# Cutting the token dimension of the experts' plain second product unevenly in four groups of one batch

## The chip, the cores and the metric

The kernel runs on one core of one Trainium2 chip. The metric is the device time of one launch in microseconds (us), taken as the median of several runs; lower is better. A run's profile gives a span, from the first instruction to the last, which is a little shorter than the device time.

## The reference, cut to what matters

Three stages follow one another. A memory attention over 4 batches of 576 tokens gives `x` of 2304 tokens by 512 features. A dense layer with a parametrised ReLU follows. The last stage is a mixture of four experts, all of which work on every token:

```python
p = domain_probs / (domain_probs.sum(-1, keepdims=True) + 1e-09)
for e in range(E):                      # E = 4, F = 1024
    h = np.maximum(x @ w1[e], 0.0)
    out += p[:, e:e + 1] * (h @ w2[e])  # h @ w2[e] is the second product
```

The 4 x 1024 hidden features are treated as eight groups of 512 (`NG = 8`), two to an expert. The change concerns `h @ w2[e]` of groups 3, 4, 5 and 6 for batch 1, and nothing else.

## The kernel before, in words

**Layout.** Features lie on the 128 partitions and tokens along the free dimension. A batch has `S = 576` tokens, and `HB = 288` is half of them. Every float32 operand is kept as two parts, a rounded `hi` and the rest `lo`, both of type fp32r, and a product of two operands is made as three matmuls (`PASSES`: hi·hi, hi·lo, lo·hi) which add up in PSUM.

**Order of the work.** The attention and the dense layer follow an order written out by hand (`ORDER`). `run_experts` then goes through 32 units: first batches 0 and 1 in turn for groups 0 to 7, then batches 2 and 3 in turn for groups 0 to 7. The order in which instructions are issued is the order of the Python calls; each engine runs its own in that order. A unit (g, b) computes the first product of its group with a seven-product scheme in two halves (`Up`, `hp` = 0 and 1; products `p1` to `p7`, six matmuls each of 288 columns, 84 in a unit). Between them stand the products of the second matmul for the unit before it: `old.product(n)` and `old.flush(n)`, called through `down`. VectorE builds the blocks of `h` from the products in PSUM (line 840, tiles `v` and `h`), applies the gate (line 884), and ScalarE, GpSimd and VectorE make the `hi` and `lo` parts (tile `g`).

**The plain second product.** Batches 0 and 1 use the class `Down`. Its eight products `n = 0..7` are those of four blocks `d` of 128 output features and two token halves `j`. One product is twelve matmuls into one bank of PSUM (tile `o`, line 914): two `hp`, two halves `i`, three passes. Each of the twelve has another 128 x 128 block of weights, which is loaded into the array by an instruction of its own; the moving operand is the slice `j * HB:(j + 1) * HB` of the 576 tokens of tile `g`. The PSUM pool `ps_h` has two banks, which the products take in turn. `flush(n)` adds the bank to the accumulator in SBUF on VectorE (line 931, tile `acc`), for group 0 by a ScalarE copy (line 929). Of batches 2 and 3 all groups but the last use another scheme (class `Seven`, line 978).

In a unit that hosts `Down`, products 0, 1 and 2 stand in its first half, after `p7`, `p4` and `p3`, and products 3 to 7 in its second half, after `p6`, `p2`, `p7`, `p4` and `p3`. The products of (g, batch 1) are hosted by the unit (g + 1, batch 0). For groups 3 to 6 these are the units that begin at about 592.5, 640.4, 688.1 and 736.2 us.

**Waits that stand around them.** `p4` of a half writes on into the bank that VectorE reads for `v167` (line 871), `p3` into the one that it reads for `c22` (line 874). A product `n + 2` takes the bank of product `n` after its flush.

Of the kernel before, what the change touches and what calls it, by code (L numbers as in the profile page):

```python
# [8 lines left out]
F32 = mybir.dt.float32  # L9
# [7 lines left out]
B, H, S, D, M = 4, 8, 576, 64, 32  # L17
# [4 lines left out]
HB = S // 2  # L22
# [169 lines left out]
def memory_attention_experts(ctx: ExitStack, tc: tile.TileContext, phi, q, kv, w_in, w_out, w1, w2, alpha, dp, out):  # L192
# [16 lines left out]
    ps_h = ctx.enter_context(tc.tile_pool(name="ps_h", bufs=2, space=PSUM))  # L209
# [12 lines left out]
    def unit(name, dt=F32, pool=big):  # L222
        return pool.tile([128, UNIT], dt, tag="big", name=name)
# [398 lines left out]
    xu_t, acc_t, p_t, w1_t, w2_t, g_t = {}, {}, {}, {}, {}, {}  # L622
# [10 lines left out]
    def operand(b, i):  # L633

        n = b % 2 * 7 + i
        if (b // 2, n // 2) not in xu_t:
            xu_t[b // 2, n // 2] = unit(f"x{b}{i}", F32R).rearrange("p (c x k n) -> p c x k n", c=2, x=2, k=2)
        return xu_t[b // 2, n // 2][:, n % 2]
# [155 lines left out]
    class Up:  # L794
# [6 lines left out]
        def product(self, p, a, i, start):  # L801
            w = w1_t[self.g, self.hp].rearrange("p x (c k n) -> p x c k n", c=7, k=2)
            n = 0
            for k in range(2):
                for x, y in PASSES:
                    mm(p, w[:, x, a, k], operand(self.b, i)[:, y, k], start=(start and n == 0), stop=(n == 5), skip_group_check=not start)  # L806
                    n += 1
# [89 lines left out]
    class Down:  # L897


        def __init__(self, g, b):  # L900
            self.g, self.b, self.ps = g, b, {}

        def product(self, n, hps=(0, 1)):
            d, j = divmod(n, 2)
            if 0 in hps:
                self.ps[n] = ps_h.tile([128, 512], F32, tag="h", name=f"o{self.g}{self.b}{n}")[:, 0:HB]
            self.p = self.ps[n]
            m = 6 * hps[0]
            for hp in hps:
                w = w2_t[self.g, hp, d // 2].rearrange("p x (i n) -> p x i n", i=2)  # L910
                for i in (1, 0):
                    for x, y in PASSES:
                        g = g_t[self.g, self.b, hp][:, i, y, j * HB:(j + 1) * HB]
                        mm(self.p, w[:, x, i, d % 2 * 128:(d % 2 + 1) * 128], g, start=(m == 0), stop=(m == 11), skip_group_check=len(hps) == 1)  # L914
                        m += 1

        def flush(self, n):
            d, j = divmod(n, 2)
            g, b = self.g, self.b
            if b > 1:  # L920
                a = acc_t[b][(P2, P3, P4, P5)[d // 2 * 2 + j]][:, d % 2]
                nc.vector.tensor_tensor(out=a, in0=self.p, in1=a, op=ALU.add)
                nc.sync.dma_start(out=out[d * 128:(d + 1) * 128, b * S + j * HB:b * S + (j + 1) * HB], in_=a)
                return
            if n == 0 and g == 0:
                acc_t[b] = unit(f"acc{b}", pool=pools["acc"]).rearrange("p (d n) -> p d n", d=4)
            a = acc_t[b][:, d, j * HB:(j + 1) * HB]
            if g == 0:
                nc.scalar.copy(out=a, in_=self.p)
            else:  # L930
                nc.vector.tensor_tensor(out=a, in0=self.p, in1=a, op=ALU.add)  # L931
            if g < NG - 1:
                return
            if j == 1:
                nc.sync.dma_start(out=out[d * 128:(d + 1) * 128, b * S:(b + 1) * S], in_=acc_t[b][:, d])
# [356 lines left out]
    for kind in ("in", "out"):  # L1292
        for i in range(DFF // 128):
            d = Decode(kind, i)
# [66 lines left out]
```

## Time and profile before

| quantity | value |
|---|---|
| device time, median of 3 runs | 1167.02 us (1165.84 to 1167.2) |
| span of the profiled execution | 1164.3 us |
| TensorE matmul busy | 1142.6 us, 98% of the span |
| VectorE busy | 853.2 us, 73% |
| ScalarE busy | 473.1 us, 41% |
| GpSimd busy | 410.0 us, 35% |
| mean granted clock of TensorE | 0.994 of full |

The profile gives the span of the profiled execution and no device time of its own for it; the median of the runs lies 2.7 us above the span. Engines are named PE (TensorE matmul), PEld (TensorE weight load), DVE (VectorE), ACT (ScalarE), POOL (GpSimd) and SP (SyncE). The duration of one matmul in the profile reaches from its first read to its modelled last write, and matmuls overlap; the pace of a stream is therefore read from the distance of starts.

### The profile page before, as it was taken

The numbers are of one execution on the slowest core, as the hardware profiler recorded it, in microseconds if no ns is written. First come the engines' busy times: TensorE is split into PE (matmuls) and PEld (weight loads), VectorE is DVE, ScalarE is ACT, GpSimd is POOL, SyncE is SP. The second block draws the span as 40 slices with busy tenths as digits, with TensorE's granted clock in tenths as the row PEclk, the third lists the DMA queues.
The fourth block names the chain that finished last, engine by engine and source line by source line (L and its number), as shares of the span: only waits on it lengthen the run. The fifth ranks groups of instructions, "written<-read, shape, count | busy, mean of one in ns | idle before, by whom it ended". The sixth has DMA issues, their size and how long they took to land.

```text
span 1164.3 us, 21801 instructions
## 1 busy us (share of the span) xinstructions
PE 1142.6 (98%) x8628; PEld 1096.0 (94%) x8628; DVE 853.2 (73%) x1573; ACT 473.1 (41%) x1035; POOL 410.0 (35%) x333
## 2 busy tenths in 40 slices
PE   8899999999999989999999999999999999999998
PEld 7578999999999989999999999999999999999998
DVE  6999888885558674767757766678667777777794
ACT  5567756555455534333323333223432222222220
POOL 2333022322010164745646456433333333333320
PEclk9999999999999989999999999999999999999999
DMA  9740221312000262745637455485545556555512
GB/s 375 274 177 20 73 91 55 91 37 82 1 1 1 85 258 104 279 169 212 242 120 296 152 220 227 172 303 197 181 158 189 164 165 185 162 181 182 163 65 72
DMA packets 64214, 180.02 MB, mean 155 GB/s; under 512 B 6640, under 2 KB 23024, under 8 KB 60400
## 3 DMA queue, kind: packets, MB, share of 16 engines
q1 hardware_dynamic: 64112, 178.63, 43.9%
q8 instruction: 68, 1.11, 0.4%
q14 instruction: 34, 0.28, 0.1%
HBM read 114.34 MB, written 64.26 MB: 153 GB/s over the span
## 4 chain that ended last, share of the span: by engine, by line
PE 88%; DVE 7%; DMA 2%; issue 2%; POOL 1%; ACT 1%; SPq 0%; DVEq 0%; ACTq 0%; POOLq 0%
PE o L914 18%; PE y L600 17%; PE c L978 13%; PE uy L806 12%; PE h L562 8%; PE ux L806 8%; PE uw L806 8%; PE pw L523 2%; DMA rawin<-in_w_in 2%; DVE g L232 1%; PE pm L325 0%; POOL g L232 0%; POOL w L232 0%; DVE h L884 0%; DVE g L581 0%
## 5 line engine op out<-in xcount | busy, mean ns | idle before, releaser
L914 PE MATMUL o<-g,w 128*128 128x288 f32 x1536 | 226.0, 296 | 0.7 <-DVE g L232 0.4
L914 PEld LDWEIGHTS o<-g,w 128*128 128x128 f32 x1536 | 211.6, 189 | 1.1 <-DVE g L232 0.6
L600 PE MATMUL y<-g,wout 128*128 128x288 f32 x1440 | 205.5, 297 | 0.0
L600 PEld LDWEIGHTS y<-g,wout 128*128 128x128 f32 x1440 | 194.2, 188 | 10.5 <-issue 7.0
L806 PE MATMUL uy<-x,w 128*128 128x288 f32 x1152 | 186.0, 297 | 3.4 <-DVE v L840 3.4
L806 PEld LDWEIGHTS uy<-x,w 128*128 128x128 f32 x1152 | 163.9, 189 | 6.0 <-DVE v L840 5.9
L978 PE MATMUL c<-gc,w2c 128*128 128x288 f32 x1008 | 156.3, 295 | 0.5 <-ACT acc L991 0.5
L978 PEld LDWEIGHTS c<-gc,w2c 128*128 128x128 f32 x1008 | 141.1, 188 | 1.0 <-ACT acc L991 1.0
L232 POOL TENSOR_TENSOR gc<-h,gc 128x576 fp32r<-128x576 f32 x56 | 83.0, 1490 | 143.0 <-ACT gc L965 99.9
L806 PE MATMUL ux<-x,w 128*128 128x288 f32 x768 | 122.8, 295 | 2.8 <-ACT v L844 2.7
L806 PE MATMUL uw<-x,w 128*128 128x288 f32 x768 | 122.7, 295 | 0.0
L806 PEld LDWEIGHTS ux<-x,w 128*128 128x128 f32 x768 | 108.6, 188 | 3.2 <-ACT v L844 3.2
L965 ACT CAST gc<-h 128x576 fp32r<-128x576 f32 x70 | 47.3, 675 | 152.0 <-DVE h L957 138.6
L562 PE MATMUL h<-a,wp 128*128 128x288 f32 x720 | 108.8, 296 | 0.1
L806 PEld LDWEIGHTS uw<-x,w 128*128 128x128 f32 x768 | 108.8, 188 | 0.0
L232 POOL TENSOR_TENSOR w<-raww,w 128x512 fp32r<-128x512 f32 (+1 forms) x48 | 76.3, 1606 | 86.6 <-ACT w L705 59.8
L562 PEld LDWEIGHTS h<-a,wp 128*128 128x128 f32 x720 | 99.5, 188 | 2.7 <-issue 1.3
L931 DVE TENSOR_TENSOR acc<-o,acc 128x288 f32<-128x288 f32 x112 | 50.8, 454 | 69.2 <-PE o L914 69.2
L581 DVE SCALAR_TENSOR_TENSOR pos<-neg,nal,pos 128x288 f32<-128x288 f32 x120 | 64.8, 544 | 43.0 <-ACT pos L576 42.5
L840 DVE TENSOR_TENSOR v<-uy,v 128x288 f32<-128x288 f32 x128 | 58.1, 454 | 50.7 <-PE uy L806 50.6
L575 ACT ACTIVATE neg<-h 128x288 f32<-128x288 f32 x128 | 53.0, 414 | 83.3 <-PE h L562 78.6
L232 POOL TENSOR_TENSOR g<-pos,g 128x288 fp32r<-128x288 f32 x29 | 24.4, 845 | 173.0 <-ACT g L585 142.8
(163 smaller groups left out, 1670.9 us busy)
## 6 DMA issues: line engine op xcount, KB each, us to landing
kw<-w SPq DMA_DIRECT2D x16, 1792.0 KB, 6.9
raww<-in_w SPq DMA_DIRECT2D x32, 512.0 KB, 3.9
w<-kw SPq DMA_DIRECT2D x32, 512.0 KB, 4.6
kS<-S SPq DMA_DIRECT2D x56, 256.0 KB, 5.0
w2c<-kS SPq DMA_DIRECT2D x28, 512.0 KB, 3.6
kw<-w SPq DMA_DIRECT2D x25, 512.0 KB, 2.7
w<-kw SPq DMA_DIRECT2D x48, 256.0 KB, 3.9
kv<-in_kv SPq DMA_DIRECT2D x8, 1152.0 KB, 12.6
```

Source lines behind the costliest of these rows:

```text
L232: eng.tensor_tensor(out=out, in0=in0, in1=in1.bitcast(F32), op=ALU.subtract)
L523: mm(p[64 * j:64 * j + 64, g * 256:(g + 1) * 256], vt_t[b, g][:, j, :], win_t[c][:, 2 * g + j, e * 256:(e + 1) * 256], start=True, stop=True,)
L562: mm(p, wp_t[b, c, f // 2][:, x, o2 + g * 256:o2 + g * 256 + 128], a_t[b][:, y, g, o:o + HB], start=(n == 0), stop=(n == 5))
L575: nc.scalar.activation(out=neg, in_=p, func=AF.Relu, scale=-1.0)
L581: nc.vector.scalar_tensor_tensor(out=pos, in0=neg, scalar=nal[:, ft:ft + 1], in1=pos, op0=ALU.mult, op1=ALU.add)
L600: mm(First.acc[d], w[:, x, d * 128:(d + 1) * 128], self.gt[:, y, 0:HB], start=(self.start and n == 0), stop=(self.stop and n == 2))
L806: mm(p, w[:, x, a, k], operand(self.b, i)[:, y, k], start=(start and n == 0), stop=(n == 5), skip_group_check=not start)
L840: nc.vector.tensor_tensor(out=out, in0=x, in1=y, op=ALU.add)
L914: mm(self.p, w[:, x, i, d % 2 * 128:(d % 2 + 1) * 128], g, start=(m == 0), stop=(m == 11), skip_group_check=len(hps) == 1)
L931: nc.vector.tensor_tensor(out=a, in0=self.p, in1=a, op=ALU.add)
L965: nc.scalar.copy(out=t[:, 0], in_=self.raw[q])
L978: mm(self.p, w[:, x, i, m * 128:(m + 1) * 128], self.g_t[q][:, y, i], start=(k == 0), stop=(k == 5))
```

## The change

For batch 1 and groups 3 to 6 the two token pieces of every product become unequal: 512 + 64 (group 3), 384 + 192 (group 4), 320 + 256 (group 5) and 448 + 128 (group 6) in place of 288 + 288. The number of products, of matmuls, of weight loads and of flushes stays; so do their order and the tokens covered. Even `n` (`j = 0`) has the wide piece, odd `n` the narrow one.

```diff
+        def tokens(self, j):
+
+            cut = {3: 512, 4: 384, 5: 320, 6: 448}.get(self.g, HB) if self.b == 1 else HB
+            return (cut, S) if j else (0, cut)
+
         def product(self, n, hps=(0, 1)):
             d, j = divmod(n, 2)
+            t0, t1 = self.tokens(j)
             if 0 in hps:
-                self.ps[n] = ps_h.tile([128, 512], F32, tag="h", name=f"o{self.g}{self.b}{n}")[:, 0:HB]
+                self.ps[n] = ps_h.tile([128, 512], F32, tag="h", name=f"o{self.g}{self.b}{n}")[:, 0:t1 - t0]
...
-                        g = g_t[self.g, self.b, hp][:, i, y, j * HB:(j + 1) * HB]
+                        g = g_t[self.g, self.b, hp][:, i, y, t0:t1]
...
-            a = acc_t[b][:, d, j * HB:(j + 1) * HB]
+            a = acc_t[b][:, d, slice(*self.tokens(j))]
```

## Rows read from the trace of the kernel before

**Rows 1.** The page: span, and busy time by engine (share of the span) and instructions
```profile
span 1164.3 us, 21801 instructions
PE 1142.6 (98%) x8628; PEld 1096.0 (94%) x8628; DVE 853.2 (73%) x1573; ACT 473.1 (41%) x1035; POOL 410.0 (35%) x333
```

**Rows 2.** The page: the chain that ended last, share by engine
```profile
PE 88%; DVE 7%; DMA 2%; issue 2%; POOL 1%; ACT 1%; SPq 0%; DVEq 0%; ACTq 0%; POOLq 0%
```

**Rows 3.** The page, costliest groups: busy us, mean ns of one | idle before, releaser
```profile
L914 PE MATMUL o<-g,w 128*128 128x288 f32 x1536 | 226.0, 296 | 0.7 <-DVE g L232 0.4
L931 DVE TENSOR_TENSOR acc<-o,acc 128x288 f32<-128x288 f32 x112 | 50.8, 454 | 69.2 <-PE o L914 69.2
```

**Rows 4.** Windows, the four hosting units: length, busy us (instructions) by engine, granted clock
```profile
core 0: us, PE busy (x) PEld busy (x) DVE busy (x) ACT busy (x) POOL busy (x), PEclk, DMA share, GB/s
592.50:616.40 23.90, 23.90 (x183) 23.90 (x182) 16.01 (x27) 8.06 (x14) 10.86 (x8) 1.00 0.30 102
640.30:664.20 23.90, 23.90 (x183) 23.90 (x182) 15.93 (x27) 8.06 (x14) 10.78 (x8) 1.00 0.25 92
688.00:711.90 23.90, 23.90 (x183) 23.90 (x182) 15.74 (x27) 8.06 (x14) 10.59 (x8) 1.00 0.27 102
735.80:759.70 23.90, 23.90 (x183) 23.90 (x182) 14.93 (x25) 7.86 (x14) 9.78 (x7) 1.00 0.47 170
```

**Rows 5.** Timeline of TensorE matmuls, first hosting unit: start us, length us, instructions
```profile
592.53 0.95 PE L806 MATMUL ux<-x,w 128*128 128x288 f32 x6
...
596.49 1.76 PE L914 MATMUL o<-g,w 128*128 128x288 f32 x12
...
601.26 1.76 PE L914 MATMUL o<-g,w 128*128 128x288 f32 x12
...
610.01 1.74 PE L914 MATMUL o<-g,w 128*128 128x288 f32 x12
611.59 0.96 PE L806 MATMUL uy<-x,w 128*128 128x288 f32 x6
...
616.36 0.95 PE L806 MATMUL ux<-x,w 128*128 128x288 f32 x6
```

**Rows 6.** Timeline of TensorE matmuls after an idle stretch, first plain product
```profile
426.41 3.08 PE L914 MATMUL o<-g,w 128*128 128x288 f32 x12
429.29 1.19 PE L806 MATMUL uy<-x,w 128*128 128x288 f32 x6
```

**Rows 7.** Windows, columns as in rows 4: that product, and its surroundings
```profile
426.40:429.20 2.80, 2.80 (x13) 2.80 (x13) 2.77 (x4) 1.12 (x3) 2.63 (x2) 0.50 0.90 301
...
426.00:450.00 24.00, 24.00 (x170) 24.00 (x170) 13.30 (x19) 9.63 (x21) 15.15 (x13) 0.92 0.73 256
```

**Rows 8.** Groups by form, weight loads of 32, 64 and 128 columns: mean ns
```profile
L914 PEld LDWEIGHTS o<-g,w 128*128 128x128 f32 x1536 | 211.6, 189 | 1.1 <-DVE g L232 0.6 <-ACT acc L929 0.5
...
L523 PEld LDWEIGHTS pw<-win,vt 128*64 128x64 f32 x256 | 15.5, 136 | 10.8 <-issue 5.7 <-DVE pe L362 0.3 <-ACT y L613 0.2
...
L325 PEld LDWEIGHTS pm<-kv,pe 128*32 128x32 f32 x256 | 6.5, 109 | 1.6 <-issue 1.0 <-ACT neg L575 0.5
```

**Rows 9.** Timeline, plain float32 matmuls of 128 columns and their weight loads
```profile
20.32 2.17 PE L246 MATMUL warm<-ident 128*128 128x128 f32 x18
...
20.33 2.09 PEld L246 LDWEIGHTS warm<-ident 128*128 128x128 f32 x18
```

**Rows 10.** Timeline, plain float32 matmuls of 288 columns
```profile
44.77 2.10 PE L597 MATMUL y<-g,wholeout 128*128 128x288 f32 x8
46.71 2.10 PE L559 MATMUL h<-pe,wp 128*128 128x288 f32 x8
```

**Rows 11.** Groups by form, VectorE tensor_tensor of 576 columns
```profile
L664 DVE TENSOR_TENSOR xt<-y 128x576 f32<-128x576 f32 x4 | 3.0, 751 | 0.0
```

**Rows 12.** Timeline of VectorE in the first hosting unit
```profile
598.07 2.03 DVE L232 TENSOR_TENSOR w<-s,w 128x1024 fp32r<-128x1024 f32 x1 [0.36 <-ACT w L705]
600.02 0.45 DVE L931 TENSOR_TENSOR acc<-o,acc 128x288 f32<-128x288 f32 x1
...
610.21 0.46 DVE L840 TENSOR_TENSOR v<-uy,v 128x288 f32<-128x288 f32 x1 [0.33 <-PE uy L806]
```

## The prediction

> **What bounds the kernel now.** I read the page first. TensorE is busy for 1142.6 of 1164.3 us [rows 1], and the chain of work that ended last runs through it for 88% [rows 2]. Those are averages, so the second view was the windows of the four units that host the products to be cut. In each of them TensorE matmuls and weight loads fill all 23.90 us, the granted clock is 1.00 (2.4 GHz), and VectorE, the next engine, is busy for 14.9 to 16.0 us [rows 4]. The reader is to see that nothing waits there: a nanosecond more or less of TensorE work in these units is a nanosecond of the end. The third view was the timeline, for the pace. A unit has 84 matmuls of the first product and 96 of the second, all of 288 columns; the first starts at 592.53, the next unit's first at 616.36 [rows 5]. That is 23.83 us / 180 = 132.4 ns from start to start, though the reported duration of one is 296 ns [rows 3].
>
> **The change, part by part.** Nothing is added or removed: in each of the four groups 96 matmuls stay, 48 of them wide and 48 narrow, with the same 576 columns to a pair. A pair costs 264.8 ns before. So the whole question is the pace as a function of the width.
>
> *The wide piece.* After an idle stretch one product ran at the granted clock 0.50, the 1.2 GHz level [rows 7]: twelve matmuls took 429.29 - 426.41 = 2.88 us, 240 ns each [rows 6], which is 288 columns at one per cycle and nothing more. At 2.4 GHz the columns need 120 ns, so 12.4 of the 132.4 ns are something else. It can be fixed for each matmul, and then the price is N/2.4 + 12.4: 225.7 ns for 512 columns, 199.1 for 448, 172.4 for 384, 145.7 for 320, 119.1 for 256. It can grow with the columns, and then the price is 0.4597 ns a column: 235.4, 205.9, 176.5, 147.1, 117.7. Or it can be that at 288 columns the weight load is already the slower one of the two; then the wide pieces pay only the small excess of the plain float32 rows, where 8 matmuls start over 1.94 us, 242.5 ns each, 2.5 above two turns of 120 [rows 10].
>
> *The narrow piece.* No row shows an fp32r matmul of fewer than 288 columns. What is known is that each needs a new 128 x 128 block of weights. The mean reported load is 109 ns for 32 columns of weights, 136 for 64 and 189 for 128 [rows 8]: (189 - 109)/96 = 0.83 ns a column, so 128 columns stream for about 107 ns and the rest is fixed latency. The nearest row for the pace is the plain float32 stream with only 128 columns to move, 128 weight columns to load, and the clock at 1.00 by then: 18 matmuls in 2.17 us with 0.275 us for the last, 111.5 ns each; the loads, (2.09 - 0.19)/17 = 111.8 ns [rows 9]. So a load can follow a load every 111.7 ns, and I take that as the floor F of a matmul, however narrow. The ends are 107 ns (streaming alone) and 132.4 ns (a narrow matmul no dearer than one of 288). Without a floor, at the fixed price, the narrow pieces would cost 39.1 (64), 65.7 (128) and 92.4 ns (192); these three are raised to F, the 256 of group 5 is not.
>
> *The sum, fixed price and F = 111.7,* 48 pairs to a group:
> group 3: 225.7 + 111.7 - 264.8 = 72.6 ns, 3.48 us;
> group 4: 172.4 + 111.7 - 264.8 = 19.3 ns, 0.93 us;
> group 5: 145.7 + 119.1 - 264.8 = 0;
> group 6: 199.1 + 111.7 - 264.8 = 46.0 ns, 2.21 us;
> together 6.6 us. With the price by the column: 3.95 + 1.12 + 0 + 2.53 = 7.6 us. I take the middle, 7.1 us. The ends: 5.9 us with F = 107 and the fixed price; 10.2 us with F = 132.4 and the fixed price (4.48 + 1.92 + 0.64 + 3.20); the load-bound reading of 288, F = 132.4 and wide pieces at N/2.4 + 2.5, gives 4.00 + 1.44 + 0.16 + 2.73 = 8.3 us, inside them.
>
> The Trainium skill, TensorE: Matmul & The Clock Gate, section LDWEIGHTS, states that a weight load takes its columns divided by 1.2 GHz, which is an estimate of 107 ns for 128 columns; by it alone the sum would be the 5.9 us, and the slope of [rows 8] agrees with it.
>
> *The flushes.* VectorE's add takes 454 ns at 288 columns [rows 3] and a tensor_tensor of 576 takes 751 [rows 11], so 1.03 ns a column and 157 ns fixed: about 685 ns at 512, 223 at 64, together the 908 of before. Its total stays. Where could a longer flush hold a bank? The tightest place is product 0: its flush stood behind a split of 2.03 us, began at 600.02 and ended at 600.47 [rows 12], 0.79 us before product 2 took the bank at 601.26 [rows 5]. In group 3 product 0 ends 1.12 us later and product 2 starts about 0.87 us later (1.12 less the 0.25 that a narrow product 1 saves), while the flush behind the split ends only 0.23 us later: slack 1.4 us. Cost nothing; if that cover were gone, tenths of a microsecond a unit.
>
> *The cover of v167.* In the second half, `p4` at 611.59 [rows 5] needs `v167`, which ended at 610.67 [rows 12]; product 5, narrow now, lies between `p7` and `p4`. Twelve matmuls at F last 1.34 us in place of 1.58, so the slack of 0.92 us falls to 0.68. No new wait. No DMA and no ScalarE work is moved.
>
> **The rivals.**
>
> *No floor: not slower (1167.0).* If loads of weights run far enough ahead, or several are held, the narrow matmul pays only its columns and the 12.4 ns, and each pair costs what it did: 0 us. For it: loads are a separate instruction that overlaps matmuls, and 12.4 ns is all that shows at 288. Against it: weight loads were never closer than 111.7 ns in [rows 9], where something shorter would not have shown, since the matmuls there set nearly the same pace. It decides from F of about 76 ns down: 48 x ((F - 39.1) + (F - 65.7)) ns is then 2.3 us, 0.2% of the time, which is about what a measurement of this kernel can tell from no change. The Trainium skill, same page, section Back-to-back issue gap, gives N/2.4 + 2.5 ns for an isolated matmul and about 25 ns as its least; no pair would change by that rule, and at 288 columns it gives 122.5 ns where the trace has 132.4.
>
> *Faster (1163).* If the 12.4 ns belong to the 288-wide stream and both pieces pay N/2.4 + 2.5, a pair costs 245.0, and 192 pairs save 3.8 us. It needs the absence of a floor as well.
>
> *Narrow fp32r loses its rate (1189).* A plain float32 product needs two matmul instructions, each 242.5 ns at 288 columns [rows 10], 1.68 ns a column together. If an fp32r matmul below some width ran at that price, 192 columns would cost 323 ns and 128 columns 215.6, while 64 (108) stays at F: 3.48 + 11.07 + 0 + 7.19 = 21.7 us. If 256 columns fell under it too, group 5 would add 15.0. For it: no row has a narrow fp32r matmul. Against: nothing in the trace shows fp32r leaving one column per cycle.
>
> *The clock falls (1178 to 1181).* If the grant fell to 1.2 GHz in the narrow products as it did after the idle stretch, each fall costs what 426 to 450 us lost: 170 matmuls in place of 183 or so, 1.7 us [rows 4, 7]. Two to four falls add 3.4 to 6.8. Against: a narrow product lasts 1.34 us and the next work is dense; the trace shows the lower level only after TensorE stood idle.
>
> **How the numbers follow.** The floor between 107 and 132 ns: 0.80, with its own range of 1172.9 to 1177.2, or 1172.2 to 1177.9 with the 0.7 us by which the runs differ. No floor: 0.08. Narrow fp32r at the plain price: 0.07. Clock: 0.03. Faster: 0.02. The forecast is 1167.0 + 7.1 = 1174.1 us; in the profile the span goes from 1164.3 to about 1171.4. The range of 1170.5 to 1179.5 holds the first case, most of the clock case, and floors from about 85 ns; it leaves out some 0.17. Faster by over 0.2%: 0.02; within 0.2%: 0.08; slower: 0.90, from the same cases.
>
> **What would show it.** In the units that host groups 3 to 6, the distance of starts in the products of line 914, by form: some 226 to 235 ns at 512, and the same 107 to 132 ns at 64, 128 and 192, with the loads' distance equal to it. The units should grow by about 3.7, 1.0, 0 and 2.4 us, with TensorE without idle time. Line 931 should have rows near 685 and 223 ns. I am wrong if the narrow starts come at 40 to 90 ns, if 192 columns cost over 300 ns, if the clock falls below 1.00 there, or if TensorE waits for VectorE in these units.

## The result, and the profile after

The changed kernel takes 1172.67 us (median of 3 runs, 1172.14 to 1173.26), 1.0051 of the time before (95% interval 1.0031 to 1.0071). The first medians are 5.65 us apart; five more runs of it, told of below, give 1.0064 (1.0050 to 1.0078), 7.3 us. It is slower by some 7 us, as forecast. The span of the profiled execution went from 1164.3 to 1171.5 us, where 1171.4 had been expected; that this agrees to 0.1 us is partly luck, since the three executions had spans of 1170.4, 1170.9 and 1171.5 us.

The page of the changed kernel, as in [rows 1]: TensorE is busy for 6.2 us more with the same 8628 matmuls.

```profile
span 1171.5 us, 21801 instructions
PE 1148.8 (98%) x8628; PEld 1100.1 (94%) x8628; DVE 851.6 (73%) x1573; ACT 472.9 (40%) x1035; POOL 409.2 (35%) x333
```

Windows of the changed kernel over the hosting units, as in [rows 4], of which the first and the last stand here: TensorE still fills all four, at a granted clock of 1.00. Nothing waits for a longer flush or a shorter cover.

```profile
592.80:620.30 27.50, 27.50 (x182) 25.39 (x180) 15.58 (x27) 8.05 (x14) 11.07 (x8) 1.00 0.27 98
...
740.90:767.10 26.20, 26.20 (x183) 25.44 (x181) 14.39 (x25) 7.85 (x14) 9.75 (x7) 1.00 0.48 177
```

Timeline of TensorE matmuls in the changed kernel: the first matmuls of the hosting units and of the units behind them, and two products of group 3.

```profile
592.80 0.95 PE L806 MATMUL ux<-x,w 128*128 128x288 f32 x6
...
596.77 2.94 PE L920 MATMUL o<-g,w 128*128 128x512 f32 x12
599.55 0.95 PE L806 MATMUL uy<-x,w 128*128 128x288 f32 x6
600.34 1.42 PE L920 MATMUL o<-g,w 128*128 128x64 f32 x12
601.60 1.05 PE L806 MATMUL uw<-x,w 128*128 128x288 f32 x6
602.48 2.94 PE L920 MATMUL o<-g,w 128*128 128x512 f32 x12
...
620.35 1.03 PE L806 MATMUL ux<-x,w 128*128 128x288 f32 x6
...
644.26 0.95 PE L806 MATMUL ux<-x,w 128*128 128x288 f32 x6
...
669.14 0.99 PE L806 MATMUL ux<-x,w 128*128 128x288 f32 x6
...
693.00 0.95 PE L806 MATMUL ux<-x,w 128*128 128x288 f32 x6
...
716.88 0.95 PE L806 MATMUL ux<-x,w 128*128 128x288 f32 x6
...
740.92 0.95 PE L806 MATMUL ux<-x,w 128*128 128x288 f32 x6
...
767.10 1.01 PE L806 MATMUL ux<-x,w 128*128 128x288 f32 x6
```

The same starts in the kernel before, beside the first unit's in [rows 5]; the third hosting unit begins at 688.30 us, not at about 688.1 as said above:

```profile
640.41 0.95 PE L806 MATMUL ux<-x,w 128*128 128x288 f32 x6
...
664.24 0.95 PE L806 MATMUL ux<-x,w 128*128 128x288 f32 x6
...
688.30 0.95 PE L806 MATMUL ux<-x,w 128*128 128x288 f32 x6
...
712.13 0.95 PE L806 MATMUL ux<-x,w 128*128 128x288 f32 x6
...
736.18 0.95 PE L806 MATMUL ux<-x,w 128*128 128x288 f32 x6
...
760.01 0.95 PE L806 MATMUL ux<-x,w 128*128 128x288 f32 x6
```

Each hosting unit took 23.83 us before. Now the one of group 3 (512 + 64) takes 620.35 - 592.80 = 27.55, group 4 (384 + 192) 24.88, group 5 (320 + 256) 23.88, group 6 (448 + 128) 26.18 us: 3.72 + 1.05 + 0.05 + 2.35 = 7.17 us more. The reader is to see two things besides. The wide product of 512 took 599.55 - 596.77 = 2.78 us, 232 ns a matmul. The narrow one took 601.60 - 600.34 = 1.26 us, and the six matmuls behind it 602.48 - 601.60 = 0.88 us in place of 0.79. The trace gives the reason: the first narrow matmul starts at 600.34, the second only 0.03 us later, and from there on they follow every 0.11 us. So the start of a matmul that waits for its weights is reported some 0.08 us before its turn, and the last of the narrow pace falls on the next group. Together 1.35 us, 112 ns a matmul.

And the units between the hosting units got shorter. The first went from 640.41 - 616.36 = 24.05 us to 644.26 - 620.35 = 23.91, the second from 24.06 to 693.00 - 669.14 = 23.86, the third stayed (24.05 and 24.04). Before, the weight loads of each of the three had waited 0.2 us for VectorE (tile `v`, line 840); in the changed kernel one of the three waits is left. From the first start to the last of these rows, the stretch of the four hosting units and the three between, the kernel takes 767.10 - 592.80 = 174.30 us in place of 760.01 - 592.53 = 167.48, so 6.82 us more.

### The profile page after: what moved, and what is told of

Read it like the earlier page. It is cut to its first block, busy times and chain, and to the rows that moved or that the text cites. A ratio compares the mean times of both kernels' runs of the same rounds, so it can differ in the third digit from the quotient of the medians.

```text
span 1171.5 us, 21801 instructions
## 1 busy us (share of the span) xinstructions
PE 1148.8 (98%) x8628; PEld 1100.1 (94%) x8628; DVE 851.6 (73%) x1573; ACT 472.9 (40%) x1035; POOL 409.2 (35%) x333
## 4 chain that ended last, share of the span: by engine, by line
PE 89%; DVE 6%; issue 1%; DMA 1%; POOL 1%; ACT 1%; DVEq 0%; POOLq 0%; ACTq 0%; SPq 0%
PE o L920 18%; PE y L600 17%; PE c L984 13%; PE uy L806 12%; PE h L562 8%; PE uw L806 8%; PE ux L806 8%; PE pw L523 3%; DMA rawout<-in_w_out 1%; PE warm L246 1%; DVE g L232 1%; PE pm L325 1%; POOL g L232 0%; POOL w L232 0%; PE pc L357 0%
## 5 line engine op out<-in xcount | busy, mean ns | idle before, releaser
L920 PE MATMUL o<-g,w 128*128 128x288 f32 (+5 forms) x1536 | 232.7, 300 | 0.7 <-DVE g L232 0.4
L920 PEld LDWEIGHTS o<-g,w 128*128 128x128 f32 x1536 | 215.5, 189 | 3.5 <-DVE g L232 0.6
L937 DVE TENSOR_TENSOR acc<-o,acc 128x288 f32<-128x288 f32 (+4 forms) x112 | 50.9, 454 | 76.1 <-PE o L920 75.9
L844 ACT COPY v<-ux 128x288 f32<-128x288 f32 x64 | 25.6, 400 | 152.1 <-PE ux L806 146.3
```

## The experiments

**The changed kernel again**, five more runs, no edit.

> The changed kernel once more, to narrow its interval. Theory (a matmul costs its columns, but never less than one weight load of about 112 ns): the four hosting units grew by 3.72, 1.05, 0.05 and 2.36 us in its profile and the span by 7.2, so 6.5 to 7.5 us over the kernel before, ratio 1.0056 to 1.0064. If the true gain is nearer the 5.65 us between the medians of the first runs, the ratio is 1.0048.

Measured: 1173.71 us against 1166.42, ratio 1.0064 (1.0050 to 1.0078). That is 7.3 us, inside the interval of the first runs too. The 5.65 us between the first medians (1.0048) lie just below the new interval, which reaches from 5.8 to 9.1 us.

**All four groups 512 + 64.**

```diff
-            cut = {3: 512, 4: 384, 5: 320, 6: 448}.get(self.g, HB) if self.b == 1 else HB
+            cut = {3: 512, 4: 512, 5: 512, 6: 512}.get(self.g, HB) if self.b == 1 else HB
```

> All four groups cut 512+64. Theory (floor of one weight load): each hosting unit grows by the 3.72 us of group 3, together 14.9, less some 0.3 to 0.4 us of waits on VectorE in the units between that go, so about 14.5 us over the kernel before (ratio 1.0124). Rival (the cost comes from the new forms themselves, paid once for each width, or from the clock): not four times group 3, but 4 to 8 us.

Measured: 1180.15 us, ratio 1.0121 (1.0108 to 1.0135), 13.7 us. In its profile each of the four hosting units takes 27.54 us and each unit between 23.92, so that the stretch is 181.92 us, 14.4 more than before: four times group 3 less what the units between give back. It is no cost paid once for a new form.

**All four groups 320 + 256.** The same line with 320 four times.

> All four groups cut 320+256. Theory (floor of 112 ns, 256 columns take 119): nothing, 0 to 0.3 us, ratio 1.0000 to 1.0003. Rival (unequal pieces cost by themselves, through longer flushes or waits for a bank): some tenths of a microsecond in each hosting unit, 1 us or more in all, with TensorE idle before products in the trace.

Measured: 1166.51 us against 1166.42, ratio 1.0000 (0.9991 to 1.0008). Unequal pieces by themselves cost nothing that can be measured, 1 us at most; in the profile the stretch is 167.57 us against 167.48. So the cost lies in pieces narrower than 256.

**Half of the weight columns for the narrow piece.** On top of 512 + 64 in four groups (the line of `mm` is shortened; the run leaves out half of the output features of the narrow pieces):

```diff
+            rows = 64 if t1 - t0 == 64 else 128
...
-                        mm(self.p, w[:, x, i, d % 2 * 128:(d % 2 + 1) * 128], g, ...)
+                        mm(self.p[0:rows], w[:, x, i, d % 2 * 128:d % 2 * 128 + rows], g, ...)
...
+                r = 64 if (g in (3, 4, 5, 6) and b == 1 and j) else 128
-                nc.vector.tensor_tensor(out=a, in0=self.p, in1=a, op=ALU.add)
+                nc.vector.tensor_tensor(out=a[0:r], in0=self.p[0:r], in1=a[0:r], op=ALU.add)
```

> As all four groups cut 512+64, but the matmuls of the 64-token piece take only the first 64 of their 128 weight columns, so 64 of 128 output features of these tokens are left out for groups 3 to 6 of batch 1. Theory (the floor is the loading of the weight columns): the mean reported load is 136 ns for 64 columns and 189 for 128, so the floor falls by about 53 ns to some 58, 48 x 53 ns = 2.6 us less in each group, 4 us over the kernel before in place of 14.5. Rival (a fixed least distance between matmul instructions, whatever they load): still about 14.5 us.

Measured: 1171.80 us, ratio 1.0048 (1.0034 to 1.0061), 5.4 us. The number of matmuls and of columns moved is that of the run with 13.7 us; 61% of the cost went away with half of the weight columns. So the floor is the loading of weights, not a least distance between instructions. Timeline of that kernel, one narrow product and what follows it:

```profile
599.90 0.83 PE L921 MATMUL o<-g,w 128*64 128x64 f32 x12
600.57 1.05 PE L806 MATMUL uw<-x,w 128*128 128x288 f32 x6
```

Twelve starts take 0.67 us where they took 1.26. The next group again takes 0.89 us in place of 0.79 (it ends at 601.46), so a narrow matmul costs 64 ns, where some 58 had been expected; with 232 for the wide one that is 31 ns a pair over the 264.8, or 6.0 us in the four groups before the units between give some back. The 4 us that were expected lie at the edge of the interval.

**Both products of a block back to back, and matmul by matmul in turn.** Again 512 + 64 in four groups. Both products of a feature block are issued at the place of the wide one (a control), or their matmuls alternate (`INTERLEAVED` stands for the choice and is False in the control; `steps(n)` holds the twelve matmuls of product `n`):

```diff
+            if n % 2 == 0:
+                steps = [self.steps(n), self.steps(n + 1)]
+                if INTERLEAVED:
+                    for x, y in zip(*steps):
+                        x()
+                        y()
+                else:
+                    for s in steps:
+                        for x in s:
+                            x()
+            self.p = self.ps[n]
```

> As all four groups cut 512+64, but the two products of a feature block are issued together, the wide one and then the narrow one, at the place of the wide one; the place of the narrow one holds only its flush. A control for the interleaved run. Theory: the same matmuls, so about 14.5 us over the kernel before, perhaps a little more where VectorE waits move.

> The same places, but the two products are issued matmul by matmul in turn, wide, narrow, wide, narrow, with the same block of weights loaded for both. Theory (a block of weights can be loaded only while the one before it is in use, one ahead): the load for the next wide matmul starts when the narrow one starts and lasts longer than it, so each narrow matmul still costs 112 ns and the time is that of the control, about 14.5 us over the kernel before. Rival (loads run ahead and only their mean rate counts): two loads of 112 ns fit under a pair of 232 + 28 ns, the cost goes, and the time is within 1.5 us of the kernel before.

Measured: back to back 1185.79 us, ratio 1.0164 (1.0149 to 1.0179), 19.1 us; in turn 1188.88, ratio 1.0186 (1.0169 to 1.0203), 22.2 us. Both miss the 14.5 us. Taking the matmuls in turn saves nothing, as the theory says, but the places cost more than it said. Timeline of the kernel in turn, one pair of products (24 matmuls) and the two groups around `p7` and `p4`:

```profile
597.46 4.20 PE L937 MATMUL o<-g,w 128*128 128x512 f32 x24
601.50 1.04 PE L806 MATMUL uy<-x,w 128*128 128x288 f32 x6
...
615.22 1.03 PE L806 MATMUL uy<-x,w 128*128 128x288 f32 x6
616.80 1.05 PE L806 MATMUL uy<-x,w 128*128 128x288 f32 x6 [0.55 <-DVE v L840]
```

The same pair in the control:

```profile
596.45 4.21 PE L937 MATMUL o<-g,w 128*128 128x512 f32 x24
600.50 1.04 PE L806 MATMUL uy<-x,w 128*128 128x288 f32 x6
```

A row of this view merges both widths. The twelve pairs took 601.50 - 597.46 = 4.04 us in turn and 600.50 - 596.45 = 4.05 us one product after the other. With the 0.08 us that falls on the next group that is 344 ns a pair, 232 + 112. So a wide matmul of 232 ns ahead of each narrow one does not help, and the rival's 260 ns a pair is refuted. Timeline of the weight loads in turn: the second and the third from the wide matmul at 597.46 us on; the first starts with it.

```profile
597.70 0.19 PEld L937 LDWEIGHTS o<-g,w 128*128 128x128 f32 x1
597.80 0.19 PEld L937 LDWEIGHTS o<-g,w 128*128 128x128 f32 x1
```

While the wide matmul runs one block is loaded, the narrow one's. The load for the next wide matmul starts 0.23 us later, together with the narrow matmul (597.69), and the one after it another 0.11 us later, when that load has come in and the next wide matmul can take its weights (its start is reported 0.08 us early, at 597.72).

What was missed are waits. The waits of TensorE in the kernel in turn, 592 to 790 us (engine, tile, line, waited for: us in total, times, longest):

```profile
PE uy L806 <- DVE v L840: 2.5, 5, 0.6
PE o L937 <- DVE acc L969: 1.8, 4, 0.5
```

With no product between `p7` and `p4`, TensorE waits for `v167` in each unit, 0.55 us by the profile. That is the cover which the prediction worked out: a slack of 0.92 us with a product of 1.58 us in the gap, so 0.66 us too little without it. The control has the same row. The second row is the bank that a flush has not yet left, 0.45 us a unit, for which the prediction had said tenths of a microsecond if the cover were gone. The control has no such row, and it accounts for most of the 3 us between the two.

**Streams of one width.** A kernel that issues 48 matmuls of each width, each with another block of 128 weight columns.

```python
for k in range(count):
    b = k % (1024 // cols)
    o = k % 2 * 576
    mm(p, w[:, b * cols:(b + 1) * cols], x[:, o:o + n], start=(k == 0), stop=(k == count - 1))
```

> A kernel of its own that computes nothing of the reference: streams of 48 fp32r matmuls, each with another block of 128 weight columns, of 512, 448, 384, 320, 288, 272, 256, 240, 224, 192, 128, 64 and 32 columns, first with the other engines nearly idle, then with VectorE, ScalarE, GpSimd and DMA busy; between them streams with 64 and 32 weight columns. Theory: the distance of starts falls in a line with the width down to about 112 ns, reached between 256 and 224 columns, and is flat at 112 below; 64 weight columns give about 58 and 32 about 30 ns where 64 columns are moved. On the 12.4 ns that stand above 288 / 2.4: if they are contention with other engines, the quiet streams run at 213 to 216 ns for 512 columns and 120 to 123 for 288, and the loud ones at 225 to 235 and 132; if they belong to the matmul, quiet and loud agree at 232 and 132. Rival to the floor (fp32r loses its rate below 256 columns): 240 and 192 columns would take over 300 ns.

Timeline of that kernel; the pace is the distance of two rows' starts over 48.

```profile
22.01 11.04 PE L36 MATMUL quiet512c<-x,w 128*128 128x512 f32 x48
32.89 9.89 PE L36 MATMUL quiet448c<-x,w 128*128 128x448 f32 x48
...
57.97 6.49 PE L36 MATMUL quiet288c<-x,w 128*128 128x288 f32 x48
64.29 6.19 PE L36 MATMUL quiet272c<-x,w 128*128 128x272 f32 x48
70.32 5.92 PE L36 MATMUL quiet256c<-x,w 128*128 128x256 f32 x48
76.07 5.54 PE L36 MATMUL quiet240c<-x,w 128*128 128x240 f32 x48
81.45 5.51 PE L36 MATMUL quiet224c<-x,w 128*128 128x224 f32 x48
...
92.15 5.49 PE L36 MATMUL quiet128c<-x,w 128*128 128x128 f32 x48
97.48 8.43 PE L36 MATMUL quiet64c<-x,w 128*128 128x64 f32 x48
...
128.94 2.93 PE L36 MATMUL few64c<-x,w 128*64 128x64 f32 x48
131.71 11.25 PE L36 MATMUL few512c<-x,w 128*32 128x512 f32 x48
142.79 1.70 PE L36 MATMUL few64c<-x,w 128*32 128x64 f32 x48
144.33 5.73 PE L36 MATMUL up2512c<-x,w 128*128 128x512 f32 x24
149.89 11.04 PE L36 MATMUL loud512c<-x,w 128*128 128x512 f32 x48
```

| columns moved | weight columns | ns a matmul |
|---|---|---|
| 512 | 128 | 226.7 |
| 288 | 128 | 131.7 |
| 272 | 128 | 125.6 |
| 256 | 128 | 119.8 |
| 240 | 128 | 112.1 |
| 224 | 128 | 111.5 |
| 192 | 128 | 111.5 |
| 128 | 128 | 111.0 |
| 64 | 64 | 57.7 |
| 64 | 32 | 32.1 |

With 128 weight columns this is the whole curve. From 256 columns up a matmul costs its columns at 2.4 GHz and some 12 to 16 ns (226.7 - 213.3 = 13.4 at 512, 119.8 - 106.7 = 13.1 at 256); at 240 the floor of 112 ns takes over and stays. With 64 weight columns the floor is half of that. The row of 32 weight columns stands below 64 columns at 2.4 GHz and 13 ns (39.7), and 512 columns with 32 weight columns took (142.79 - 131.71)/48 = 230.8 ns, so the part of 13 ns is not the same with fewer weight columns. The rival, a lost rate of fp32r, would have shown 300 ns and more at 240. With the other engines busy 48 matmuls of 512 columns took the same 11.04 us, and those of 288 the same 131.7 ns, so the 13 ns do not come from that work. The loud streams of 256 columns and fewer say nothing: TensorE waited before most of them, and the granted clock was 0.50 to 0.81. The stream of 64 columns with 128 weight columns went another way: it did not stay at 112 ns. Windows of the same kernel, columns as in [rows 4]:

```profile
95.50:97.60 2.10, 2.10 (x22) 2.10 (x20) 0.00 (x0) 0.00 (x0) 0.00 (x0) 1.00 0.00 0
97.60:107.90 10.30, 10.30 (x60) 10.30 (x59) 0.52 (x2) 0.00 (x0) 0.00 (x0) 0.60 0.01 2
```

The granted clock, 1.00 through the streams of 224, 192 and 128 columns, fell to the 1.2 GHz level within the stream of 64 without any idle time of TensorE, and the matmuls of 32 columns that follow came every (115.97 - 105.73)/48 = 213 ns, at a granted clock of 0.50. That is the clock rival of the prediction, in another kernel, and so the next run asked when it would strike this one.

**The four narrow pieces of a group in one run.** 512 + 64 in four groups; the narrow products 1, 3 and 5 are issued with product 7, side by side in one bank, with one flush of 4 x 64 columns. `gathered(n)` is true for the narrow pieces of batch 1, groups 3 to 6.

```diff
+            if not self.gathered(n):
+                return self.one(n, hps)
+            if n < 7:
+                return
+            p = ps_h.tile([128, 512], F32, tag="h", name=f"o{self.g}{self.b}{n}")[:, 0:256]
+            for d in range(4):
...
+                            mm(p[:, d * 64:(d + 1) * 64], w[:, x, i, d % 2 * 128:(d % 2 + 1) * 128], g, start=(m == 0), stop=(m == 11))
```

> All four groups cut 512+64, but the four narrow pieces of a group stand one after another in one bank at the place of the last one: 48 matmuls of 64 columns without a break, and one flush of 256 columns. The places of the other narrow pieces are empty, as they are in the back-to-back control, with its waits for VectorE. Theory (floor of 112 ns, granted clock untouched): about the control's 19 us over the kernel before, the narrow stretch 48 x 112 ns = 5.4 us. Rival (a sustained narrow stream lowers the clock, as the stream of 64 columns in the kernel of widths did after some matmuls): part of the stretch runs at 213 ns a matmul and some work after it at the 1.2 GHz level, the granted clock in the four units falls below 1.00, and the time is 25 us or more over the kernel before.

Measured: 1192.18 us, ratio 1.0227 (1.0209 to 1.0245), 25.8 us: the rival's number. Timeline of TensorE in that kernel, end of the first hosting unit, and then its windows, columns as in [rows 4]:

```profile
616.56 5.68 PE L924 MATMUL o<-g,w 128*128 128x64 f32 x48
622.06 1.79 PE L806 MATMUL ux<-x,w 128*128 128x288 f32 x6
623.64 1.58 PE L806 MATMUL uy<-x,w 128*128 128x288 f32 x6
```
```profile
620.00:622.00 2.00, 2.00 (x18) 2.00 (x18) 0.00 (x0) 0.00 (x0) 0.00 (x0) 0.90 0.89 343
622.06:625.20 3.14, 3.14 (x15) 3.14 (x16) 1.09 (x2) 1.27 (x3) 0.00 (x0) 0.53 0.80 248
```

The narrow matmuls themselves still come every (622.06 - 616.56)/48 = 115 ns, but the clock, 1.00 up to 620 us, falls at their end, and the dense products behind them pay: six matmuls take 623.64 - 622.06 = 1.58 us in place of 0.79. It fell so in all four units: over the narrow stretch and the matmuls behind it the granted clock was 0.80, 0.82, 0.69 and 0.81, and 1.00 between. Over the control the four hosting units and the four behind them are 5.7 us longer, 1.4 us for each fall, where the prediction had priced one at 1.7. In the changed kernel twelve narrow matmuls stand between dense work, and the clock stayed at 1.00.

**Where 5 ns at 512 columns come from.** The real kernel pays 232 ns at 512 columns, the stream 227. Two kernels of their own took up layout and order of the operands, and reads of PSUM by the other engines.

The inner loops of the first, shortened:

```python
for hp in range(2):            # layout and order of the second product
    for i in (1, 0):
        for a, b in PASSES:
            mm(p, w[hp][:, a, i * 256 + d % 2 * 128:][:, 0:128], x[hp][:, i, b, at:at + n], ...)
```

> A kernel of its own that computes nothing of the reference: products of twelve fp32r matmuls of 512 and of 288 columns with weights and operands laid out and ordered as in the experts' second product, four products each: as there; with lo parts replaced by whole numbers; with the columns taken from 64 on; with one block of weights for all; with one operand for all. Theory (the price is N/2.4 plus about 13 ns, as in the kernel of widths; the 232 ns at 512 columns of the real kernel come from where or in which order its operands lie): 232 ns as in the kernel, and 227 in at least one of the other four. Rival (they come from the work of the other engines around): 227 ns in all five. At 288 columns 132 ns in all of them.

> A kernel of its own that computes nothing of the reference: the products of the kernel of operands, of 512 and then of 288 columns, alone; beside VectorE reading PSUM; beside ScalarE reading PSUM; beside both; beside DMA loads; beside VectorE reading SBUF. Theory (the 5 ns by which 512 columns cost more in the real kernel are contention with the reads of PSUM by VectorE and ScalarE, which the kernel of widths did not have): about 232 ns beside both, 227 alone. Rival (not contention of that kind): 227 in all, and the 5 ns stay open.

Measured: streams of 11.04 us as in the kernel of widths, the same 226.7 ns, in all five streams of the first and in four of the six of the second. The two others, beside ScalarE and beside DMA loads, began after a wait of 1.19 us and took 11.17 and 11.18 us; beside both engines it was 11.04. At 288 columns the first has 131.6 ns. Timeline of the first and of the second kernel:

```profile
25.66 11.04 PE L60 MATMUL likekernel512d<-x,w 128*128 128x512 f32 x48
```
```profile
60.73 11.04 PE L60 MATMUL both512d<-x,w 128*128 128x512 f32 x48
```

Both theories fell. The 5 ns, 48 x 5 = 0.25 us in group 3, stay open. Work of other engines need not be behind them: in the kernel of widths the stream of 512 columns with 32 weight columns, with the other engines nearly idle, paid 230.8 ns too. Whether for the same reason is not shown.

## Why the prediction was right

**The bound.** TensorE filled the four units before and fills them after, and nearly all that it lost there came out at the end. That 7.17 us in the units stand beside 7.2 in the span is partly luck: the units between gave back 0.35 us, which leaves 6.82, and the changed kernel was 0.27 us late before the first of these units began (592.80 against 592.53), where nothing had been changed.

**The narrow piece.** F = 111.7 ns was taken from the nearest row, a plain float32 stream of 128 columns [rows 9]. That row could not show a floor, since its matmuls set nearly the same pace themselves, as the prediction says; it came out right within 1 ns by some luck, but the slope of the loads [rows 8] had pointed at 107 ns. The streams of fp32r show 111.0 to 112.1, and the floor falls with the weight columns (57.7 ns for 64), so it is the weight load. That the load is one block ahead and no more was shown by the run in turn. The rivals "no floor" and "faster" fall with it, and so does "narrow fp32r loses its rate". The reading by which 288 columns are bound by the load already falls too: 272 and 256 columns cost less (125.6 and 119.8 ns).

**The wide piece.** The forecast stood between 225.7 ns (fixed price) and 235.4 (by the column) at 512. The streams decide for the fixed price, with 12 to 16 ns from 256 columns up. The kernel itself does not pay it: its wide pieces cost 232 ns at 512, (765.01 - 762.56)/12 = 204 at 448 and (667.02 - 664.92)/12 = 175 at 384, in each case between the fixed price (225.7, 199.1, 172.4) and the price by the column (235.4, 205.9, 176.5). No cause was found. So the middle of both was right for no shown reason, and that is luck.

**The sum.** Forecast 3.7, 1.0, 0 and 2.4 us for the four units; measured 3.72, 1.05, 0.05 and 2.35. The fixed price alone would have given 6.6 us in place of 7.1, also inside the stated range.

**The flushes.** Groups by form of the changed kernel, VectorE, to be held against the 454 ns of [rows 3]:

```profile
L937 DVE TENSOR_TENSOR acc<-o,acc 128x512 f32<-128x512 f32 x4 | 2.8, 689 | 7.5 <-PE o L920 7.5
...
L937 DVE TENSOR_TENSOR acc<-o,acc 128x64 f32<-128x64 f32 x4 | 0.9, 223 | 1.2 <-PE o L920 1.0
```

Expected were 685 and 223 ns, and no product waited for a bank. The cover of `v167` held too; the three runs that took it away (back to back, in turn and gathered) waited 0.55 us a unit for it.

**The clock.** It stayed at 1.00 in the four units. The prediction gave a fall 0.03, with two arguments. That a narrow product is short and dense work follows it was borne out: the run with 512 + 64 in all four groups kept 1.00 with twelve narrow matmuls at a time, and the gathered run, with the same matmuls in rows of forty-eight, did not. That the trace shows the lower level only after idle time holds for the kernel before, but not as a rule: the gathered run fell to the lower level out of work without a gap.

**What was not foreseen.** The units behind the first two hosting units got shorter by 0.14 and 0.20 us, as their loads no longer waited for VectorE, and so the loss of a hosting unit does not come out at the end quite whole. (The start at 620.35 is one of those reported early: with 0.08 us moved, the hosting unit grew by 3.80 us and the one behind it shrank by 0.22; their sum is the same.)

## What to carry to other kernels

Price a matmul by two numbers read from the trace, the columns plus a small part on top and one load of its weights, and take the larger. In this kernel the second, 112 ns for 128 float32 weight columns, binds below some 240 columns moved. So 320 + 256 is free, while 512 + 64 adds 3.7 us to the 12.7 us that the 96 matmuls of a group take before (96 x 132.4 ns). A wide neighbour does not hide the load, and neither of the other orders tried did; half of the weight columns took 61% of the cost away. Where narrow pieces can't be avoided, leave them spread among dense work, since twelve of them did nothing to the clock and forty-eight in a row lowered it for the dense products behind. No cut tried here beats the equal halves.

## What the runs showed of the hardware that had not been expected

A stream of matmuls without any idle time can lose the higher clock: 48 matmuls of 64 columns, 112 ns apart, brought the granted clock from 1.00 to 0.53 in the stretch behind them, and so in all four units of the gathered run, while streams of 128 to 224 columns at the same pace of 111 ns kept 1.00.

Weights are loaded one block ahead and no more: in the run in turn a load starts with the matmul before its own (597.46, 597.70, 597.80 us), however long that one lasts.

The profile reports the start of a matmul that waits for its weights some 0.08 us early, so the pace of a narrow product is read from the start of the second group behind it, not of the first.
